# P transposes of every second macro step as pairs of 64-row tiles beside the K transposes, in a two-block cached attention kernel

## The chip, the cores and the metric

The kernel runs on one core of one Trainium2 chip. The metric is the device time of one execution in microseconds (us); lower is better. Three executions of the kernel before took 855.37, 857.67 and 857.76 us, median 857.67.

A core has a matrix engine (TensorE, PE; its weight loads are shown apart as PEld), a vector engine (VectorE, DVE), a scalar engine (ScalarE, ACT), GpSimd (POOL) and SyncE (SP), which here issues the loads. PSUM is the memory that TensorE writes; the kernel uses it as 8 banks of 512 fp32 (or 1024 bf16) per partition.

## The reference

Two independent attention blocks A and B, with the same shapes and all inputs in bf16; their outputs are joined along the last axis.

```
B, Sq, D = 16, 64, 640 ;  H, Sk, Dh = 32, 512, 128
q      = (x @ wq).reshape(B, Sq, H, Dh).transpose(0, 2, 1, 3)
scores = einsum("bhqd,bhkd->bhqk", q, k_cache) * Dh ** -0.5
p      = softmax(scores, axis=-1)
o      = einsum("bhqk,bhkd->bhqd", p, v_cache)
out    = o.transpose(0, 2, 1, 3).reshape(B, Sq, H * Dh) @ wo
```

The K and V caches of the two blocks, four arrays of 64 MB, make nearly all of the 297 MB that the DMA engines move.

## The kernel before

**Tiling.** Two batches (64 queries each) stand together on the 128 partitions. A *step* g is one head of such a batch pair; a *macro step* m is two steps (two heads), and there are 256 of them; a *pair* is two macro steps, m even and m odd, and there are 128. Heads are worked on in four passes of 16 heads (two per block), each over 8 batch pairs.

**Kinds of operations.** Each operation of the plan has a short name; `em_<name>` emits its instructions.

- KX (TensorE) transposes the K tile of a macro step: 32 transposes of 64-row tiles, alternating between partitions 0 to 63 and 64 to 127 and between two PSUM banks (6 and 7). KE (DVE) copies both banks to SBUF.
- QJ, QZ, QN (TensorE) compute the projected queries, 5 matmuls over 640 = 5 x 128; QEJ, QEZ, QEN (ACT) copy them out. QZ is for the first pass over the heads, QN for the rest; the last 16 pairs have none.
- SM (TensorE) computes the scores of one step, in bank 2 + g % 4. MX (DVE) takes the row maximum, EX (ACT) the exponential with the row sum, RC2 (DVE) two reciprocals, NM (POOL) the normalised P of one step in bf16 (`pn_ring`).
- TR2 (TensorE) transposes the normalised P of a macro step, 2 steps x 4 column tiles: 8 transposes of 128x128 into one bank, `TRB[m % 2]`, so bank 2 for even and bank 3 for odd macro steps. TA2 (ACT, even m) or TE2 (DVE, odd m) copies the 1024 columns to `pT_ring`.
- PV2 (TensorE) multiplies with V, 16 matmuls of 64 columns, each for one batch (j), step (sub) and column tile (t), in bank 1; OE4 (ACT) copies a pair's result out.
- OP2 and OX (TensorE) multiply with `wo`, 512 and 128 output columns, in banks 0 and 4; OX runs every fourth pair for 16 heads' worth of its small columns. OVP, OXP (ACT) and OVF, OXF (DVE) copy or add the sums, ST stores. XT and XTE transpose x of block B, through bank 4.

Banks 2 to 5 are thus shared: scores, P transposes (2 and 3), OX and XT (4).

**Order.** It is written out by hand as a table. `PHASES` has four phases, from pair 0, 16, 112 and two before the end, and for each engine (TensorE, ACT, DVE, POOL) a list of entries (kind, offset in macro steps, sub, time within a period). `build_plan` gives each operation the time stamp m - offset + 2 t / PERIOD and sorts every engine's list by it; a template's times order the work and are no durations. Dependencies are found from the resources (banks and ring slots) that an operation reads and writes, in the order of the time stamps, and become semaphore waits; `prune_waits` drops those that another one implies.

**Loads.** All K, V and weight loads are issued by SP in one list. `LEAD` and `WLEAD` say how many macro steps ahead of its first use a load is wanted, and `STEP_US`, `DMA_US`, `START_US` and `BEFORE` turn the plan into a pace: each load waits for the TensorE operation that this pace puts beside it. K has a ring of 9 macro steps, V one of 5 pairs; each of the two V loads of a pair is 512 KB, as is each K load.

In the steady part of the plan (pairs 16 to 111), TensorE's order in a pair is SM x4, KX, QN, TR2 x2 (16 transposes), OP2 x2 (4 matmuls), KX, PV2 x2, with OX or XT between OP2 and the second KX where they occur.

Lines of the kernel before that the profile names: L550 K transposes, L557 their copy, L567 Q, L596 scores, L605 maxima, L621 exponentials, L627 reciprocals, L635 normalisation, L644 P transposes, L651 and L656 their copies by DVE and ACT, L666 PV, L681 and L691 output matmuls.

Of the kernel before, what the change touches and what calls it, by code (L numbers as in the profile page):

```python
# [15 lines left out]
class Cfg:  # L16
# [6 lines left out]
    LEAD = 4.68  # L23
    WLEAD = 4.56
    STEP_US = ((8, 39.85), (32, 17.16), (256, 3.11))
    DMA_US = dict(LDK=1.40, LDV=1.44, LDWQ=1.8, LDWO=1.8, LDX=1.3, LDXR=0.5)
    START_US = -168.79
    BEFORE = 1.75
# [17 lines left out]
          ("QEZ", 0, 1, 2.19), ("QEJ", 2, 0, 2.79), ("EX", 1, 0, 3.02), ("QEN", -6, 0, 3.12), ("TA2", -2, 0, 3.58),  # L46
          ("QEZ", 0, 2, 4.2), ("EX", 1, 1, 4.36), ("XTE", 8, 0, 4.4), ("QEZ", 0, 3, 4.6), ("QEZ", 0, 4, 4.7),
          ("OVP", -3, 0, 5.0), ("QEZ", 0, 5, 5.61), ("OXP", -3, 0, 5.75), ("QEZ", 0, 6, 5.9), ("QEZ", 0, 7, 6.3)),
# [10 lines left out]
          ("QEN", -6, 0, 3.35), ("TA2", -2, 0, 3.59), ("EX", 1, 1, 4.45), ("OXP", -3, 0, 4.84), ("OVP", -3, 0, 4.86),  # L59
          ("XTE", 0, 0, 4.88)),  # L60
         (("KE", 3, 0, 0.04), ("RC2", -1, 0, 0.64), ("MX", 0, 0, 0.87), ("MX", 0, 1, 1.32), ("MX", 1, 0, 1.41),
          ("MX", 1, 1, 1.55), ("KE", 2, 0, 2.37), ("RC2", 0, 0, 3.49), ("TE2", -1, 0, 4.58), ("OXF", -3, 0, 5.55),
          ("OVF", -3, 0, 5.65)),
# [21 lines left out]
    )  # L85
    TRB = (2, 3)
    OXB = 4
    OXH = False
    KTB = (6, 6)
# [23 lines left out]
def build_plan(dims, cfg):  # L113
# [72 lines left out]
    def make_op(kind, m, sub, ts):  # L186
# [64 lines left out]
        if kind in ("TE2", "TA2"):  # L251
            return mk("dve" if kind == "TE2" else "act", kind, m, [], [bank(cfg.TRB[m % 2]), ("pT", m % cfg.NT)], ts)
# [631 lines left out]
```

## Time and profile before

| | before |
|---|---|
| median of three executions | 857.67 us |
| the profiled execution, time / span | 857.66 / 855.9 us |
| PE, DVE, ACT, POOL busy | 805.9, 726.6, 633.0, 418.0 us |
| moved by DMA | 297.13 MB, mean 347 GB/s |
| K transposes, L550 | 8192, PE busy 167.4 us |
| P transposes, L644 | 2048, PE busy 137.4 us |
| granted TensorE clock | 1.00 |

The span is the time from the first to the last instruction; the execution's own time has 1.8 us around it. A line of costly groups reads: source line, engine, operation, output <- inputs, shapes, count | busy us, mean ns of one | idle time of the engine before them, and what ended it. A line of the timeline reads: start and length in us, engine, line, operation, tiles, shapes, count, and in brackets an idle stretch before it. Matmuls overlap in a pipeline, so the length of one (about 190 to 390 ns) is more than what it adds; what a group adds is the distance from its start to that of the next group. Some matmul records are missing from the trace: 497 of 512 for L681, for instance.

### The profile page before, as it was taken

What the parts mean: (1) busy time and instruction counts of PE and PEld (TensorE: products, weight loads), DVE (VectorE), ACT (ScalarE), POOL (GpSimd) and SP (SyncE); (2) the same over time, 40 slices, a digit from 0 to 9 for tenths busy, and PEclk for the clock granted to TensorE, in tenths of its full rate; (3) what the DMA queues carried; (4) which work ended last, traced back from release to release, by engine and by line L of the source; (5) the groups of instructions that cost most, each with busy time, mean ns of one, the idle gap of its engine ahead of it and who ended that gap; (6) DMA issues with size and microseconds to landing.
All of it is one profiled execution on the core that took longest, in us unless ns stands there. A gap on an engine that the chain in (4) does not pass through costs nothing.

```text
span 855.9 us, 38296 instructions
## 1 busy us (share of the span) xinstructions
PE 805.9 (94%) x16953; PEld 561.8 (66%) x17084; DVE 726.6 (85%) x1184; ACT 633.0 (74%) x1450; POOL 418.0 (49%) x518
## 2 busy tenths in 40 slices
PE   5999999999999999999999899999999999999987
PEld 3566666666666766766666666666676666666665
DVE  3588888898888899898898788988888889889995
ACT  2677787787787777777777777777877867767775
POOL 0344554545544554554554445555455545446554
DMA  8999999999999999999999999999999999999993
GB/s 266 321 368 367 357 352 328 358 352 346 356 363 354 355 364 366 359 368 369 366 354 368 316 355 364 360 358 362 355 363 364 364 360 370 346 307 350 368 352 115
DMA packets 232581, 297.13 MB, mean 347 GB/s; under 512 B 14304, under 2 KB 166880, under 8 KB 232416
## 3 DMA queue, kind: packets, MB, share of 16 engines
q1 hardware_dynamic: 230112, 292.06, 100.2%
q8 instruction: 133, 2.18, 1.1%
q10 hardware_dynamic: 2304, 2.62, 0.9%
q14 instruction: 32, 0.26, 0.1%
HBM read 290.72 MB, written 2.62 MB: 343 GB/s over the span
## 4 chain that ended last, share of the span: by engine, by line
PE 81%; DMA 9%; DVE 3%; issue 3%; ACT 2%; POOL 1%; SPq 1%; POOLq 0%; ACTq 0%; DVEq 0%
PE ps L550 15%; PE ps L567 14%; PE ps L666 14%; PE ps L596 13%; PE ps L644 11%; PE ps L681 11%; DMA v_ring<-in_B_v_cache_dram 6%; PE ps L691 3%; DMA v_ring<-in_A_v_cache_dram 3%; DVE ktp_ring L557 2%; DVE negmax L605 1%; POOL pn_ring L635 1%; ACT p_ring L621 1%; DMA wq_sb<-in_A_wq_dram 1%; ACT pT_ring L656 1%
## 5 line engine op out<-in xcount | busy, mean ns | idle before, releaser
L635 POOL TENSOR_SCALAR pn_ring<-p_ring,recip 128x512 bf16<-128x512 bf16 x512 | 417.4, 846 | 429.9 <-DVE recip L627 403.2
L621 ACT ACTIVATE p_ring<-ps,negmax 128x512 bf16<-128x512 f32 x512 | 350.0, 689 | 77.5 <-DVE negmax L605 74.3
L557 DVE COPY ktp_ring<-ps 128x2048 bf16<-128x2048 bf16 x256 | 311.9, 1218 | 78.6 <-PE ps L550 78.3
L605 DVE TENSOR_REDUCE negmax<-ps 128x1 f32<-128x512 f32 x512 | 320.6, 683 | 19.7 <-PE ps L596 12.6
L550 PEld LDWEIGHTS ps<-ident,kn_ring 64*128 64x128 bf16 x8192 | 135.8, 95 | 99.2 <-issue 58.8
L550 PE MATMUL ps<-ident,kn_ring 64*128 64x64 bf16 x8192 | 167.4, 191 | 5.3 <-DVE ktp_ring L557 2.6
L673 ACT ACTIVATE oT_ring<-ps 128x512 bf16<-128x512 f32 x128 | 76.4, 597 | 123.7 <-PE ps L666 123.7
L567 PE MATMUL ps<-xT_sb,wq_sb 128*128 128x512 bf16 (+2 forms) x544 | 135.7, 376 | 26.8 <-issue 18.3
L666 PE MATMUL ps<-pT_ring,v_ring 128*128 128x64 bf16 x4096 | 142.7, 193 | 7.4 <-DMA v_ring<-in_B_v_cache_dram 4.1
L644 PEld LDWEIGHTS ps<-ident,pn_ring 128*128 128x128 bf16 x2048 | 124.9, 98 | 34.8 <-ACT p_ring L621 3.4
L644 PE MATMUL ps<-ident,pn_ring 128*128 128x128 bf16 x2048 | 137.4, 219 | 1.7 <-POOL pn_ring L635 1.2
L596 PE MATMUL ps<-ktp_ring,qc_ring 128*64 128x512 bf16 x1024 | 137.6, 387 | 1.2 <-issue 1.1
L666 PEld LDWEIGHTS ps<-pT_ring,v_ring 128*128 128x128 bf16 x4096 | 127.4, 98 | 15.9 <-DMA v_ring<-in_B_v_cache_dram 5.3
L681 PE MATMUL ps<-wo_sb,oT_ring 128*128 128x512 bf16 x497 | 132.1, 379 | 5.0 <-ACT pT_ring L656 2.5
L656 ACT ACTIVATE pT_ring<-ps 128x1024 bf16<-128x1024 bf16 x128 | 132.6, 1036 | 0.6 <-PE ps L644 0.4
L621 ACT ACTIVATION_READ_ACCUMULATOR p_ring<-ps,negmax 128x1 f32 x512 | 105.2, 206 | 0.0
L567 PEld LDWEIGHTS ps<-xT_sb,wq_sb 128*128 128x128 bf16 x660 | 54.9, 99 | 62.8 <-DMA wq_sb<-in_A_wq_dram 7.7
L651 DVE COPY pT_ring<-ps 128x1024 bf16<-128x1024 bf16 x128 | 86.3, 674 | 6.9 <-PE ps L644 6.8
L583 ACT ACTIVATE qc_ring<-ps 128x512 bf16<-128x512 f32 (+1 forms) x129 | 77.1, 597 | 14.2 <-PE ps L567 14.2
L596 PEld LDWEIGHTS ps<-ktp_ring,qc_ring 128*64 128x64 bf16 x1024 | 47.3, 109 | 37.4 <-issue 5.0
L681 PEld LDWEIGHTS ps<-wo_sb,oT_ring 128*128 128x128 bf16 x512 | 43.4, 98 | 31.8 <-ACT pT_ring L656 4.6
L627 DVE RECIPROCAL recip<-rowsum 128x2 f32<-128x2 f32 x256 | 39.9, 156 | 9.1 <-ACT p_ring L621 9.1
(16 smaller groups left out, 109.1 us busy)
## 6 DMA issues: line engine op xcount, KB each, us to landing
kn_ring<-in_A_k_cache_dram SPq DMA_DIRECT2D x128, 512.0 KB, 6.7
v_ring<-in_A_v_cache_dram SPq DMA_DIRECT2D x128, 512.0 KB, 6.6
kn_ring<-in_B_k_cache_dram SPq DMA_DIRECT2D x128, 512.0 KB, 6.4
v_ring<-in_B_v_cache_dram SPq DMA_DIRECT2D x128, 512.0 KB, 6.3
wq_sb<-in_A_wq_dram SPq DMA_DIRECT2D x8, 640.0 KB, 6.6
wo_sb<-in_A_wo_dram SPq DMA_DIRECT2D x8, 640.0 KB, 6.8
wq_sb<-in_B_wq_dram SPq DMA_DIRECT2D x8, 640.0 KB, 6.4
wo_sb<-in_B_wo_dram SPq DMA_DIRECT2D x8, 640.0 KB, 7.4
```

Source lines behind the costliest of these rows:

```text
L550: last = e.transpose(kt_ps[hs][:, 64 * t:64 * t + 64], kn_ring[r, m % NKB, t // 8, t % 8 * DH:(t % 8 + 1) * DH], ident[r, r])
L557: ins = e.tensor_copy(ktp_ring[:, ktslot(op.idx)], ps[:, b:b + 2, :].rearrange("p b s -> p (b s)").bitcast(BF16))
L567: last = e.matmul(dst[:, col:col + n], wq_sb[:, qslot(hh // G), kt, (hh % G) * DH:(hh % G + 1) * DH], xT_sb[:, kt, lo * 128:hi * 128], sta ...
L596: ins = e.matmul(s_bank(g)[64 * j:64 * j + 64, :], q[:, 64 * j:64 * j + 64], kt[:, sub, j], start=True, stop=True, tile_position=(0, 64 * j))
L605: ins = e.reduce_max(negmax[:, r:r + 1], s_bank(g), axis=AX.X, negate=True)
L621: ins = e.activation(p_ring[:, g % NP, :], s_bank(g), ACTF.Exp, bias=negmax[:, r:r + 1], scale=1.0, accum_out=rowsum[:, r:r + 1])
L635: ins = e.tensor_scalar(dst, src, recip[:, r:r + 1], 1.0, ALU.mult, ALU.mult)
L644: ins = e.transpose(pt_flat(m)[:, (4 * sub + t) * 128:(4 * sub + t + 1) * 128], pn_ring[:, g % NPN, t * 128:(t + 1) * 128], ident[:, :])
L651: ins = e.tensor_copy(pT_ring[:, m % NT].rearrange("p s t q -> p (s t q)"), pt_flat(m))
L656: ins = e.activation(pT_ring[:, m % NT].rearrange("p s t q -> p (s t q)"), pt_flat(m), ACTF.Copy)
L666: ins = e.matmul(qo_ps[:, col:col + 64], v_ring[:, m // 2 % NVP, j, 2 * (m % 2) + sub, t * DH:(t + 1) * DH], pT_ring[:, m % NT, sub, t, 64 ...
L681: ins = e.matmul(out_ps, oT_ring[:, m // 2 % NO, 2 * (m % 2) + sub, :], wo_sb[:, wslot(ps_, hh // G), hh % G, 0:N0], start=(hh == 0), stop ...
```

## The change

Three things change.

First, `TRB` becomes `((2,), (3, 4))`. For even macro steps nothing changes. For odd ones a P transpose of 128x128 becomes two transposes of 64 rows, one per batch j, with a 64x64 identity: sixteen in place of eight. Batch 0 goes to bank 3 and batch 1 to bank 4, each half a bank. The DVE copy (TE2) reads both half banks as one access pattern and writes `pT_ring` batch by batch; PV2 reads it in that layout for odd m.

Second, the four phases of `PHASES` are written anew. In the steady part TensorE's order in a pair is now SM x4, KX, QN, TR2 (even, 8 transposes), OP2 (2 matmuls), TR2 (odd, 16 half transposes), KX, OP2 (2 matmuls), PV2 x2, with OX and XT between the last OP2 and PV2. DVE's order becomes KE, MX, RC2, MX, MX, KE, MX, TE2, RC2, where it was KE, RC2, MX x4, KE, RC2, TE2. ACT keeps three EX, QEN, TA2, EX, OE4. POOL's four normalisations are permuted.

Third, the constants of the loads' pace change, and at the very start a K tile is loaded and transposed ahead of the first x and wq. Two kinds that no phase uses (MX2 and RC4) are removed.

```diff
-    LEAD = 4.68
-    WLEAD = 4.56
-    STEP_US = ((8, 39.85), (32, 17.16), (256, 3.11))
+    LEAD = 4.6
+    WLEAD = 4.51
+    STEP_US = ((8, 47.78), (32, 9.16), (256, 3.09))
...
-    START_US = -168.79
-    BEFORE = 1.75
+    START_US = -120.72
+    BEFORE = 2.51
...
         (16,
-         (("SM", 0, 0, 0.0), ("SM", 0, 1, 0.21), ("SM", 1, 0, 0.43), ("SM", 1, 1, 0.64), ("KX", 2, 0, 1.42),
-          ("QN", -6, 0, 2.07), ("TR2", -2, 0, 2.96), ("TR2", -1, 0, 3.76), ("OP2", -4, 0, 3.83),
-          ("OP2", -3, 0, 3.98), ("XT", 0, 0, 4.35), ("OX", -3, 0, 4.75), ("KX", 5, 0, 4.88), ("PV2", -2, 0, 5.52),
-          ("PV2", -1, 0, 6.09)),
...
+         (("SM", 0, 0, 0.0), ("SM", 0, 1, 0.21), ("SM", 1, 0, 0.43), ("SM", 1, 1, 0.64), ("KX", 2, 0, 1.03),
+          ("QN", -6, 0, 2.41), ("TR2", -2, 0, 3.07), ("OP2", -4, 0, 3.1), ("TR2", -1, 0, 3.81), ("KX", 5, 0, 4.31),
+          ("OP2", -3, 0, 4.65), ("OX", -3, 0, 5.14), ("XT", 0, 0, 5.48), ("PV2", -2, 0, 5.49), ("PV2", -1, 0, 6.14)),
...
-    TRB = (2, 3)
+    TRB = ((2,), (3, 4))
...
-            return mk("pe", "TR2", m, [("pn", g0 % cfg.NPN), ("pn", g1 % cfg.NPN), ("ident",)], [bank(cfg.TRB[m % 2])],
-                      ts)
+            return mk("pe", "TR2", m, [("pn", g0 % cfg.NPN), ("pn", g1 % cfg.NPN), ("ident",)],
+                      [bank(b) for b in cfg.TRB[m % 2]], ts)
...
+        def pt_bank(m):
+            b = cfg.TRB[m % 2]
+            return ps[:, b[0]:b[-1] + 1, :].bitcast(BF16)[:, :, 0:8 * 128 // len(b)]
+
+        def pt_copy(m):
+            return pT_ring[:, m % NT].rearrange("p (b c) -> p b c", b=len(cfg.TRB[m % 2]))
...
             for sub in range(2):
-                g = 2 * m + sub
                 for t in range(4):
-                    ins = e.transpose(pt_flat(m)[:, (4 * sub + t) * 128:(4 * sub + t + 1) * 128], pn_ring[:, g % NPN, t * 128:(t + 1) * 128], ident[:, :])
...
+                    src = pn_ring[:, (2 * m + sub) % NPN, t * 128:(t + 1) * 128]
+                    for j in range(2 if pairs else 1):
+                        n = 64 if pairs else 128
+                        r = slice(n * j, n * j + n)
+                        c = (4 * sub + t) * n
+                        last = e.transpose(dst[:, j, c:c + n], src[r], ident[r, r])
+                        first = first or last
...
-            ins = e.tensor_copy(pT_ring[:, m % NT].rearrange("p s t q -> p (s t q)"), pt_flat(m))
+            ins = e.tensor_copy(pt_copy(op.idx), pt_bank(op.idx))
...
-                                       pT_ring[:, m % NT, sub, t, 64 * j:64 * j + 64], start=(t == 0), stop=(t == 3))
+                                       pT[:, sub, t, j], start=(t == 0), stop=(t == 3))
```

More of the change, by code (lines that the diff above doesn't have):

```diff
@@ L236, in make_op @@
             return mk("act", kind, idx, [], [bank(b)] + [("qc", c_) for c_ in cells], ts, aux=cells)
-        if kind == "MX2":
-            return mk("dve", "MX2", m, [], [bank(2 + g0 % cfg.NS), bank(2 + g1 % cfg.NS), ("negmax", r0), ("negmax", r1)],
-                      ts)
-        if kind == "RC4":
-            rs = [g % cfg.NR for g in range(4 * k, 4 * k + 4)]
-            return mk("dve", "RC4", k, [("rowsum", r) for r in rs], [("recip", r) for r in rs], ts)
         if kind == "SM":
@@ L517, in mha_kernel @@
         pn_ring = sb("pn_ring", [128, NPN, SK], BF16)
-        pT_ring = sb("pT_ring", [128, NT, 2, 4, 128], BF16)
+        pT_ring = sb("pT_ring", [128, NT, 2 * 4 * 128], BF16)
         oT_ring = sb("oT_ring", [128, NO, 4, 128], BF16)
@@ L639, in em_TR2 @@
             m = op.idx
+            pairs = len(cfg.TRB[m % 2]) > 1
+            dst = pt_bank(m)
             first = last = None
             for sub in range(2):
-                g = 2 * m + sub
                 for t in range(4):
-                    ins = e.transpose(pt_flat(m)[:, (4 * sub + t) * 128:(4 * sub + t + 1) * 128], pn_ring[:, g % NPN, t * 128:(t + 1) * 128], ident[:, :])
-                    first = first or ins
-                    last = ins
+                    src = pn_ring[:, (2 * m + sub) % NPN, t * 128:(t + 1) * 128]
[5 more added lines that the diff above has]
+                        first = first or last
             return first, last
         def em_TE2(e, op):
-            m = op.idx
-            ins = e.tensor_copy(pT_ring[:, m % NT].rearrange("p s t q -> p (s t q)"), pt_flat(m))
+            ins = e.tensor_copy(pt_copy(op.idx), pt_bank(op.idx))
             return ins, ins
         def em_TA2(e, op):
-            m = op.idx
-            ins = e.activation(pT_ring[:, m % NT].rearrange("p s t q -> p (s t q)"), pt_flat(m), ACTF.Copy)
+            ins = e.activation(pt_copy(op.idx), pt_bank(op.idx), ACTF.Copy)
             return ins, ins
@@ L660, in em_PV2 @@
             m = op.idx
+            pT = pT_ring[:, m % NT]
+            if len(cfg.TRB[m % 2]) > 1:
+                pT = pT.rearrange("p (j s t q) -> p s t j q", j=2, s=2, t=4)
+            else:
+                pT = pT.rearrange("p (s t j q) -> p s t j q", j=2, s=2, t=4)
             first = last = None
```

34 lines of the change are left out of this document (12 added, 22 removed), and 58 rows, old and new, of the table PHASES.

## The prediction

> **What bounds the kernel now.** I read the busy table first, then the chain of work that ended last, the costliest groups, the order of time inside one repetition, and last the long stretch of repetitions in one window.
>
> ```profile
> span 855.9 us, 38296 instructions
> PE 805.9 (94%) x16953; PEld 561.8 (66%) x17084; DVE 726.6 (85%) x1184; ACT 633.0 (74%) x1450; POOL 418.0 (49%) x518
> PE 81%; DMA 9%; DVE 3%; issue 3%; ACT 2%; POOL 1%; SPq 1%; POOLq 0%; ACTq 0%; DVEq 0%
> L550 PEld LDWEIGHTS ps<-ident,kn_ring 64*128 64x128 bf16 x8192 | 135.8, 95 | 99.2 <-issue 58.8
> L644 PEld LDWEIGHTS ps<-ident,pn_ring 128*128 128x128 bf16 x2048 | 124.9, 98 | 34.8 <-ACT p_ring L621 3.4
> ```
>
> TensorE (PE) is busy 94% of the span and is 81% of the chain, with DMA second at 9%. The two weight-load rows are for the K transposes (L550, 64-row tiles) and the P transposes (L644, full tiles).
>
> One repetition (two macro steps, a "pair") in order of time, with TensorE alone:
>
> ```profile
> 428.56 1.05 PE L596 MATMUL ps<-ktp_ring,qc_ring 128*64 128x512 bf16 x8
> 429.55 0.64 PE L550 MATMUL ps<-ident,kn_ring 64*128 64x64 bf16 x32
> 430.35 1.03 PE L567 MATMUL ps<-xT_sb,wq_sb 128*128 128x512 bf16 x4 [0.16 <-issue]
> 431.21 1.06 PE L644 MATMUL ps<-ident,pn_ring 128*128 128x128 bf16 x16
> 432.10 1.03 PE L681 MATMUL ps<-wo_sb,oT_ring 128*128 128x512 bf16 x4
> 433.06 0.64 PE L550 MATMUL ps<-ident,kn_ring 64*128 64x64 bf16 x32
> 433.64 1.11 PE L666 MATMUL ps<-pT_ring,v_ring 128*128 128x64 bf16 x32
> 434.67 0.62 PE L596 MATMUL ps<-ktp_ring,qc_ring 128*64 128x512 bf16 x4
> ```
>
> Start to start, a pair takes 434.67 - 428.56 = 6.11 us with no hole. (The Q row shows 4 of its 5 matmuls; the 0.16 stands where a record is missing, since 429.55 + 0.57 + 5 x 0.218 = 431.21.) Of it 16 P transposes take 432.10 - 431.21 = 0.89, so 55.6 ns each, and 32 K transposes 433.64 - 433.06 = 0.58 or, in the chain, 0.57: 17.8 ns each, every one with a weight load of its own.
>
> ```profile
> 52.70:730.80 678.10, 653.14 (x13901) 458.53 (x14003) 593.49 (x966) 519.49 (x1195) 342.85 (x420) 1.00 1.04 358
> 360.00:420.00 60.00, 58.06 (x1240) 41.16 (x1248) 53.35 (x88) 46.90 (x108) 30.74 (x38) 1.00 1.07 368
> 730.80:846.00 115.20, 105.81 (x2320) 74.23 (x2337) 105.73 (x179) 84.70 (x195) 60.81 (x76) 1.00 0.97 329
> PE ps L666 <- DMA v_ring<-in_B_v_cache_dram: 4.1, 7, 1.2
> PE ps L666 <- DMA v_ring<-in_A_v_cache_dram: 1.7, 3, 1.2
> ```
>
> Window rows give, after the length, busy time of PE, PEld, DVE, ACT and POOL, then clock, DMA share and GB/s. The first is the long middle: 105 pairs (L644 has 1680 instructions there, 16 a pair). PE is busy 653 of 678 us; V loads that have not landed hold PE for 4.1 + 1.7 = 5.8 us in it (the two wait rows, of the same window). DMA moves 358 GB/s x 678.1 us = 242.8 MB there; in the second window it holds 368 GB/s for 60 us. So the middle could not be shorter than 242.8 / 0.368 = 660 us: TensorE bounds it, with the transfers 18 us behind.
>
> **The change, part by part.**
>
> *P transposes of the odd step.* Eight 128x128 transposes (0.445 us) become sixteen of 64 rows. They have the shape of the K transposes: 64x128 weights, a 64x64 identity, alternating halves, two banks. At 17.8 ns they take 0.285: 0.16 us less a pair. The bounds: 0.285 if the halves overlap as K's do; 16 x 27.8 (half of 55.6) = 0.445, nothing saved, if they follow one another. I take K's rate, the same form beside them.
>
> The number of weight loads doubles, and a load of 64 rows takes 95 ns against 98 for 128 (the two L550 and L644 rows above). Eight more of them, if nothing hid them, would cost 8 x 0.095 = 0.76 us a pair, and the change would be a loss of 0.76 - 0.16 = 0.6. But 32 K loads pass in 0.57 us, so loads of this form overlap; I take 0 and keep the loss as a rival. The Trainium skill, "TensorE: Matmul & The Clock Gate", section "LDWEIGHTS (loading the stationary operand)", states it as a rule: a weight load's time goes by its columns, not its rows; the 95 and 98 ns agree, and by the rule without overlap the sum would be that loss.
>
> *Order on TensorE.* Now: scores, K, Q, 8 P, 2 output matmuls, 16 half P, K, the other 2, PV. There is still one passage from 512-column matmuls into 64-row tiles at this place: before, the output group takes 433.06 - 432.10 = 0.96 for 4 x 0.218, so the passage costs 0.09, and it only moves. Leaving K for output matmuls is new here; the last repetitions already do it with no hole (K at 790.43 + 0.57, two outputs 0.44, P at 791.44). So 0, at most 0.09 a pair. The new pair: 6.11 - 0.16 = 5.95.
>
> *Evacuation.* ACT's copy of the even step keeps form (1036 ns). DVE's 674 ns copy reads two half banks instead of one. Near row: K's copy reads two banks, 2048 elements in 1218 ns, no dearer per element. Far row: two 683 ns reductions of 512 fp32 = 1.37 us. I take 674. DVE per pair, start to start: 2 x 1.13 (K) + 2.38 (4 maxima) + 0.15 (2 reciprocals) + 0.6 = 5.4 of 5.95, still covered; it would stop being cover above some 1.15 us.
>
> *Waits that move.* Half P now needs banks 3 and 4, so exponentials 2 and 3 of the pair. These end 2.7 and 3.4 us after the first score matmul (430.58 + 0.68 and 431.24 + 0.69, less 428.56), and half P starts at 0.99 + 0.57 + 1.09 + 0.445 + 0.53 (two outputs and the passage) = 3.6: 0.2 in hand. K, two outputs and PV would queue behind it; I take 0, at most the 0.1 of the next wait. DVE does maximum 4 after a K copy instead of before, so exponential 4 comes later, but ACT does it after the pT copy anyway. That pT copy ends at 433.42, 0.22 before PV (433.64). PV now comes 0.16 earlier and ACT's chain 0.07 at most (a reciprocal moves behind the first maximum): 0.05 to 0.13 in hand. I take 0; the bound is 0.1 a pair, 10.5 us. The small output matmuls (26 groups of 0.89) lose the K group between them and the scores that reuse bank 4; DVE's 0.29 or ACT's 0.28 still fits before the third score matmul, 1.5 us later. POOL, half idle (342.85 of 678), only permutes its work: nothing.
>
> *SP's loads.* Order differs in the first 19 only: a K tile goes ahead of x and Wq. PE waited 7.7 us for Wq; it may wait 1.4 longer (512 KB at 368 GB/s), and may gain 0.96 of K transposes and a 1.32 us wait for their copy. I take 0, since transfers run at 366 GB/s until 100 us and set the pace. Leads and paces shift by some per cent; V loads land a median 6.5 us after issue, with a lead in steps that shrinks with the pair.
>
> *Last repetitions* (730.8 on): no Q, pairs at 5.49 us against 4.9 of PE work, DVE busy 105.7 of 115.2 us. They are not TensorE's: 0.
>
> *Sum.* 105 x 0.16 = 16.8. The middle falls to 661.3, against 660 for the transfers; with the cover down from 18 us to 1, V waits must grow. I give back half the present 5.8, so 3: middle 664.3, which is 365.5 GB/s. Span 855.9 - 16.8 + 3 = 842.1; the profiled execution took 857.66 (1.8 around the span), as good as the median 857.67. So **844 us**.
>
> **The rivals.**
>
> 1. The pT wait opens: PV finds ACT 0.1 late in every pair. 857.7 - 16.8 + 10.5 = 851.4. For it: the thin 0.05 to 0.13. Against: ACT is idle 23% of the middle.
> 2. Down to the transfer floor: new pacing removes the V waits, middle 660 (-18), and the waits for the pT copy at 742 and 749 us (0.56 and 0.74) go: 857.7 - 18 - 1.3 = 838. Against: 368 GB/s without a pause.
> 3. No change, 857.7, in one of three ways. The half tiles don't overlap (0.445 us; 0.05): against it stands K's rate. The two-bank copy goes to 1.2 us or more and DVE takes the place of PE (0.02). Or the transfers cannot average above the 358 GB/s of the middle, which then stays at 678 us (0.04): 368 over 60 us speaks against it. The Trainium skill, "DMA: Bandwidth & Descriptors", section "Specifications", gives about 358 GB/s as HBM's limit per core, and by that figure nothing would be won; the 60 us at 368 disagree.
> 4. Slower: V starvation. From 466 to 482 us three pairs in a row had V 0.9 to 1.2 us late. A pair of the middle takes 678.1 / 105 = 6.46 us on average and its transfers 660 / 105 = 6.29, so 0.17 us a pair refills the lead after such a spell; after the change 0.01 is left. If the lead stays empty, with one such wait of 1.2 us every 4 pairs, 26 in all, 31 us come on top: 857.7 - 16.8 + 31 = 872. It decides from 0.16 us of V wait a pair. For it: at 65.7 us, with DMA at 367 GB/s, PE already waited 0.37 for V. Against: a V wait itself lets DMA catch up.
> 5. Unhidden weight loads: 857.7 + 105 x 0.6 = 921. K's rate all but excludes it.
>
> **How the numbers follow.** Chances: forecast 0.45 (own range 839 to 849), rival 1 0.17, rival 2 0.10, rival 3 0.11, rival 4 0.16, rival 5 0.01. A change under 0.3%, 2.6 us, is about what a measurement here cannot tell from none. Faster: 0.45 + 0.17 + 0.10 = 0.72; same: 0.11; slower: 0.17. The range leaves out most of rival 4 and rival 5 (0.15) and the far end of rival 2, where the start gains too (0.04): 834 to 861.
>
> **What would show it.** Right: the 16 half P matmuls in 0.28 to 0.29 us, pairs of 5.95, the middle's DMA at 364 GB/s or above, V waits up a few us. Wrong: half P at 0.45; PV waiting for the pT copy in most pairs (rival 1); V waits over 20 us (rival 4); DVE's copy above 1 us (rival 3). What would make the forecast wrong as a whole is the start: the first loads are reordered, and the trace of before shows no such order.

## The result, and the profile after

| | before | after |
|---|---|---|
| median of 4 executions each, same chip | 856.52 us | 879.63 us |
| ratio, 95% interval | | 1.028 (1.024 to 1.031) |
| profiled execution, time / span | 857.66 / 855.9 us | 883.32 / 881.5 us |
| pairs 4 to 109 (the middle) | 678.1 us | 700.0 us |
| start / last repetitions | 52.7 / 125.1 us | 53.6 / 127.9 us |

The change costs 23 us; the forecast was a gain of 14. The profiled execution of after is 3.7 us above its median, and 60 us of it (480 to 520 and 580 to 600) ran at a granted clock of 0.91, so part of these 3.7 us may be the clock's. Of the 25.6 us between the two spans 21.9 lie in the middle.

The page of after, in the order of the lines shown of before (span, busy table, chain by engine, K weight loads, and from the answer by forms the weight loads of the half tiles):

```profile
span 881.5 us, 40136 instructions
PE 774.2 (88%) x17863; PEld 534.0 (61%) x18108; DVE 723.6 (82%) x1184; ACT 635.4 (72%) x1450; POOL 415.8 (47%) x518
PE 50%; ACT 21%; DMA 12%; DVE 8%; issue 6%; SPq 2%; ACTq 0%
L549 PEld LDWEIGHTS ps<-ident,kn_ring 64*128 64x128 bf16 x8192 | 139.8, 96 | 78.4 <-issue 72.4
...
L639 PEld LDWEIGHTS ps<-ident,pn_ring 64*128 64x128 bf16 x2048 | 37.5, 95 | 59.0 <-ACT p_ring L610 47.6 <-issue 10.0 <-ACT pT_ring L648 0.6
```

TensorE is recorded as busy for less time (774 against 806 us) and the span is longer: it waits. Some 18 of these 32 us are no work saved: 114 more matmul records are missing than in before (18108 - 17863 against 17084 - 16953), and each leaves a place of 0.16 us. In the chain ACT went from 2% to 21%, DMA from 9 to 12%, "issue" from 3 to 6%. The page counts 1840 instructions more.

The timeline of after, TensorE alone, one pair and the start of the next:

```profile
435.87 1.05 PE L595 MATMUL ps<-ktp_ring,qc_ring 128*64 128x512 bf16 x8
436.86 0.64 PE L549 MATMUL ps<-ident,kn_ring 64*128 64x64 bf16 x32
439.31 1.04 PE L566 MATMUL ps<-xT_sb,wq_sb 128*128 128x512 bf16 x4 [1.80 <-issue]
440.18 0.61 PE L639 MATMUL ps<-ident,pn_ring 128*128 128x128 bf16 x8
440.63 0.59 PE L678 MATMUL ps<-wo_sb,oT_ring 128*128 128x512 bf16 x2
441.15 0.41 PE L639 MATMUL ps<-ident,pn_ring 64*128 64x64 bf16 x16
441.40 0.63 PE L549 MATMUL ps<-ident,kn_ring 64*128 64x64 bf16 x32
442.19 0.38 PE L678 MATMUL ps<-wo_sb,oT_ring 128*128 128x512 bf16 x1 [0.16 <-issue]
442.40 1.10 PE L663 MATMUL ps<-pT_ring,v_ring 128*128 128x64 bf16 x32
443.43 1.05 PE L595 MATMUL ps<-ktp_ring,qc_ring 128*64 128x512 bf16 x8
```

The 16 half P transposes take 441.40 - 441.15 = 0.25 us, 15.6 ns each, where K's 32 take 0.57, 17.8 each. The tiles are no faster than K's: within a group both follow each other at 14.5 ns, and K's 0.57 us holds some 0.1 us of passage into the full tiles behind it, which half P, with K right behind, does not have. But in this pair of 7.56 us TensorE stood still for 1.80 us ahead of Q, and nothing that the trace records released it ("issue"). The packet records of the DMA engines have what came just before: a packet of the instruction queue (16 KB) had landed 1.39 us before the end of that hole. In the table of the DMA queues for the stretch from 436.70 to 438.00 us (packets, MB, share of 16 engines) it is this line:

```profile
q8 instruction: 1, 0.02, 5.5%
```

The middle in one window (columns as before), then TensorE's waits in it (total us, times, longest), then two queues of the page, and last the instruction queue of the page of before:

```profile
53.60:753.60 700.00, 625.74 (x14635) 436.31 (x14843) 590.23 (x964) 522.36 (x1195) 339.40 (x419) 0.99 1.02 346
...
PE ps L678 <- ACT pT_ring L648: 18.7, 60, 0.6
PE ps L566 <- issue: 18.5, 105, 1.8
PE ps L549 <- issue: 10.3, 17, 1.8
PE ps L663 <- DMA v_ring<-in_B_v_cache_dram: 9.2, 10, 2.5
PE ps L663 <- DMA v_ring<-in_A_v_cache_dram: 3.4, 3, 1.3
PE ps L678 <- issue: 8.7, 45, 1.7
...
q1 hardware_dynamic: 230112, 292.06, 98.3%
q8 instruction: 141, 2.31, 1.1%
...
q8 instruction: 133, 2.18, 1.1%
```

Three waits grew.

- **V loads**: 9.2 + 3.4 = 12.6 us, against 5.8 before.
- **The pT copy of ACT**: 60 pairs. Each of these lines also covers 0.16 us of a missing matmul record (the first of the two L678 matmuls is missing in every pair, as the timeline shows), so 18.7 - 60 x 0.16 = 9 us are waiting.
- **"issue"**: the places of missing records (0.16 us each) make most of the short ones, so I count those of 0.19 us or more: 32 with 19.5 us, against 4 with 1.7 us before. Of the 32, 30 end between 1.1 and 1.75 us after an instruction packet has landed; packets come every 6 us or so, hence chance would put one in ten there. I call these 30 (18.9 us) *fetch stalls* below.

That is 7 + 9 + 17 = 33 us more, against 105 x 0.20 = 21 saved in the half tiles: 12 of the 21.9. The other 10 lie in stretches too short to name and, as far as the profiled run goes, in the lower clock.

The page of after has 141 instruction packets where before has 133. By the Trainium skill, "Perfetto Trace Analysis", section "The 4-stage abstract model", an instruction has 64 bytes. As an estimate from that, 16 more a pair (8 transposes, 8 weight loads) are 105 x 1 KB = 6.6 packets in the middle. The trace agrees: its records show 116 there for 110.

The trace also has a sharper sign than the distance from a packet. Over the whole run the half tiles add 8 transposes and 8 weight loads to each of 128 pairs, 2048 instructions, for 8 more packets: 256 to a packet, or 128 weight loads with their matmuls. In all 30 fetch stalls of after, the number of weight loads begun when the hole opened is 95 more than a multiple of 128; for the two other holes it is 104 and 40. So whenever TensorE stalls, it does so at one and the same place of its 256 instructions, whatever operation stands there, and goes on soon after a packet has landed. Before's 4 stalls stand at the same 95.

### The profile page after: what moved, and what is told of

Read it like the earlier page. It is cut to its first block, busy times and chain, and to the rows that moved or that the text cites. A ratio compares the mean times of both kernels' runs of the same rounds, so it can differ in the third digit from the quotient of the medians.

```text
span 881.5 us, 40136 instructions
## 1 busy us (share of the span) xinstructions
PE 774.2 (88%) x17863; PEld 534.0 (61%) x18108; DVE 723.6 (82%) x1184; ACT 635.4 (72%) x1450; POOL 415.8 (47%) x518
## 4 chain that ended last, share of the span: by engine, by line
PE 50%; ACT 21%; DMA 12%; DVE 8%; issue 6%; SPq 2%; ACTq 0%
ACT p_ring L610 13%; PE ps L663 12%; DMA v_ring<-in_B_v_cache_dram 9%; PE ps L595 8%; PE ps L566 8%; PE ps L549 7%; PE ps L678 7%; DVE negmax L604 5%; ACT pT_ring L648 5%; PE ps L639 5%; ACT qc_ring L582 3%; PE ps L688 3%; DMA v_ring<-in_A_v_cache_dram 2%; DVE ktp_ring L556 2%; SPq L761 1%
## 5 line engine op out<-in xcount | busy, mean ns | idle before, releaser
L604 DVE TENSOR_REDUCE negmax<-ps 128x1 f32<-128x512 f32 x512 | 334.2, 682 | 93.9 <-PE ps L595 93.6
L549 PE MATMUL ps<-ident,kn_ring 64*128 64x64 bf16 x8192 | 171.3, 191 | 20.6 <-issue 14.4
L549 PEld LDWEIGHTS ps<-ident,kn_ring 64*128 64x128 bf16 x8192 | 139.8, 96 | 78.4 <-issue 72.4
L639 PEld LDWEIGHTS ps<-ident,pn_ring 64*128 64x128 bf16 (+1 forms) x3072 | 104.7, 96 | 90.0 <-ACT p_ring L610 49.3
L566 PE MATMUL ps<-xT_sb,wq_sb 128*128 128x512 bf16 (+2 forms) x544 | 136.4, 377 | 25.3 <-issue 19.8
L663 PEld LDWEIGHTS ps<-pT_ring,v_ring 128*128 128x128 bf16 x4096 | 135.2, 98 | 33.9 <-DMA v_ring<-in_B_v_cache_dram 12.3
L678 PE MATMUL ps<-wo_sb,oT_ring 128*128 128x512 bf16 x383 | 125.7, 382 | 33.4 <-ACT pT_ring L648 19.5
L639 PE MATMUL ps<-ident,pn_ring 64*128 64x64 bf16 (+1 forms) x3072 | 132.0, 201 | 5.8 <-ACT p_ring L610 4.1
L644 DVE COPY pT_ring<-ps 128x1024 bf16<-128x1024 bf16 x128 | 88.4, 691 | 19.7 <-PE ps L639 19.4
L582 ACT ACTIVATE qc_ring<-ps 128x512 bf16<-128x512 f32 x129 | 76.9, 596 | 29.4 <-PE ps L566 29.0
L566 PEld LDWEIGHTS ps<-xT_sb,wq_sb 128*128 128x128 bf16 x660 | 54.6, 100 | 62.8 <-issue 5.8
L678 PEld LDWEIGHTS ps<-wo_sb,oT_ring 128*128 128x128 bf16 x512 | 39.4, 97 | 33.0 <-ACT pT_ring L648 16.9
```

The source lines that it names most:

```text
L549: last = e.transpose(kt_ps[hs][:, 64 * t:64 * t + 64], kn_ring[r, m % NKB, t // 8, t % 8 * DH:(t % 8 + 1) * DH], ident[r, r])
L566: last = e.matmul(dst[:, col:col + n], wq_sb[:, qslot(hh // G), kt, (hh % G) * DH:(hh % G + 1) * DH], xT_sb[:, kt, lo * 128:hi * 128], sta ...
L582: last = e.activation(qc_ring[:, c[0]:c[-1] + 1:c[1] - c[0], :], src[:, i * 128:(i + n) * 128].rearrange("p (b q) -> p b q", b=n), ACTF.Co ...
L604: ins = e.reduce_max(negmax[:, r:r + 1], s_bank(g), axis=AX.X, negate=True)
L639: last = e.transpose(dst[:, j, c:c + n], src[r], ident[r, r])
L663: ins = e.matmul(qo_ps[:, col:col + 64], v_ring[:, m // 2 % NVP, j, 2 * (m % 2) + sub, t * DH:(t + 1) * DH], pT[:, sub, t, j], start=(t == ...
```

## The experiments

Times are medians; each run ran on one of three chips beside the kernel before, which took 856.1 to 857.9 us there, so a difference of two runs is good to some 2 us. The columns from "middle" on are those of the one profiled execution, which lies up to 4 us from its median. "Stalls" are fetch stalls, "V" the waits for V loads, "copy" those for the pT copy (places of missing records taken off), all in the middle, in us. Of the fifteen totals only those of e9, e13 and e15 fell inside a range that I had given, and e10 and e12 missed one by less than 0.5 us; the argument rests on differences between runs and on the waits in their traces.

| | what | median | ratio (95%) | middle | shortest / median pair | stalls | V | copy |
|---|---|---|---|---|---|---|---|---|
| before | | 856.5 | | 678.1 | 6.11 / 6.11 | 1.7 | 5.8 | |
| after | | 879.6 | 1.028 (1.024-1.031) | 700.0 | 6.06 / 6.34 | 18.9 | 12.6 | 9 |
| e1 | full tiles | 862.9 | 1.009 (1.006-1.012) | 682.5 | 6.11 / 6.11 | 1.3 | 9 | 0 |
| e5 | full tiles, old pace: order alone | 856.7 | 1.000 (0.998-1.002) | 677.4 | 6.11 / 6.11 | 1.5 | 5.4 | 0 |
| e3 | half tiles, old pace | 867.3 | 1.012 (1.009-1.015) | 680.4 | 6.06 / 6.18 | 12.8 | 5.2 | 10 |
| e6 | before, new pace | 873.2 | 1.018 (1.015-1.021) | 692.9 | 6.11 / 6.11 | 1.6 | 19.7 | |
| e2 | before, half tiles | 888.4 | 1.038 (1.035-1.040) | 700.4 | 6.11 / 6.33 | 4.3 | 2.8 | |
| e4 | after, half loads | 834.1 | 0.974 (0.972-0.976) | 658.5 | 6.06 / 6.06 | 0.9 | 0 | 11 |
| e13 | e1, half loads | 843.6 | 0.986 (0.984-0.988) | 668.1 | 6.11 / 6.11 | 0 | 0 | 0 |
| e7 | e1, 8 more instructions a pair | 890.1 | 1.037 (1.033-1.042) | 705.3 | 6.11 / 6.48 | 9.9 | 11.4 | 0 |
| e11 | e7, half loads | 856.5 | 1.001 (1.000-1.002) | 679.1 | 6.11 / 6.25 | 0.2 | 0 | |
| e12 | e3, 8 K transposes a pair less | 851.6 | 0.995 (0.993-0.997) | 672.6 | 6.06 / 6.11 | 6.1 | 6.6 | |
| e15 | e3, half as many half tiles | 863.0 | 1.009 (1.007-1.011) | 682.0 | 6.06 / 6.22 | 8.5 | 4.4 | 4.5 |
| e9 | before, loads earlier | 857.5 | 1.001 (0.999-1.002) | 677.0 | 6.11 / 6.18 | 3.3 | 1.8 | |
| e10 | e3, loads earlier | 866.8 | 1.013 (1.011-1.014) | 685.5 | 6.06 / 6.18 | 21.9 | 2.6 | |
| e8 | e3, copies swapped | 884.5 | 1.031 (1.028-1.034) | 696.7 | 6.03 / 6.47 | 24.6 | 3.3 | 6 (DVE) |
| e14 | e8, DVE's copy earlier | 881.5 | 1.030 (1.026-1.034) | 695.2 | 5.90 / 6.47 | 27.0 | 3.6 | 0 |

### Which part costs: tiles, order, pace

**e1: after without the half tiles.**

```diff
-    TRB = ((2,), (3, 4))
+    TRB = ((2,), (3,))
```

> The changed kernel with its new order and pace, and only the half tiles undone (eight full P transposes in the odd step too, bank 3). In the profile of the changed kernel three costs stand in the middle stretch of 105 pairs: TensorE waits of 18.7 us for the pT copy of ACT, 18.9 us in which TensorE ran out of nothing that a semaphore shows and went on 1.2 to 1.6 us after a packet of the instruction queue had landed, and 12.7 us for V loads. Theory A (instruction supply suffers from the half tiles, which add 16 instructions to the 258 of a pair and make TensorE burn through them faster): the instruction waits fall back to about 2 us, a pair is TensorE's again at 6.09, time 855 to 861. Theory B (the new order and pace do the damage, whatever the tiles): instruction and V waits stay above 25 us together, time 870 to 882.

862.9 us: 16.8 less than after, and still slower than before. The stalls go from 18.9 to 1.3. So the half tiles themselves are the larger part of the loss, and something else is lost too.

**e3: after with before's pace; e5: e1 with before's pace; e6: before with the new pace.** The edit is the same five constants each time (in e6 the other way round).

```diff
-    LEAD = 4.6
-    WLEAD = 4.51
-    STEP_US = ((8, 47.78), (32, 9.16), (256, 3.09))
+    LEAD = 4.68
+    WLEAD = 4.56
+    STEP_US = ((8, 39.85), (32, 17.16), (256, 3.11))
...
-    START_US = -120.72
-    BEFORE = 2.51
+    START_US = -168.79
+    BEFORE = 1.75
```

> The changed kernel with the five constants of the loads' pace as they were before. If the pace is what makes V late, the V waits of the middle fall from 12.7 us towards 6.1 and the time to 870 to 874, with the waits for the pT copy (18.7) and for instructions (18.9) where they are. If the pace is not the cause (V is late because TensorE runs ahead between its other waits, or because DMA has no spare), V waits stay at 10 to 15 us and the time within 876 to 883.

> The new order alone: eight full P transposes in the odd step, and the five constants of the loads' pace as before. Measured so far: changed kernel 879.6, its pace undone 867.3, its half tiles undone 862.9, before 856.3. If the two costs add (pace 12, half tiles 17), the order by itself gives 851 to 854, a little faster than before or the same. If the pace only hurts where half tiles speed TensorE up, this comes out at 860 to 863. In both cases the pair is 6.11 with waits for the pT copy of about 0.1 us inside it.

> The kernel before with only the five constants of the loads' pace of the changed one. If the pace by itself makes loads late, V waits in the middle rise from 6 to 10 us or more and the time is 860 to 868. If it hurts only with the new order, the time stays within 854 to 859.

The order alone costs nothing (856.7). Half tiles on top cost 867.3 - 856.7 = 10.6, and the pace 879.6 - 867.3 = 12.3: together the 23 of the change. In the old order the pace alone costs 873.2 - 857.9 (before, beside it) = 15.3, and its profile shows where. TensorE's waits in the middle of e6:

```profile
PE ps L567 <- issue: 16.7, 105, 0.2
PE ps L666 <- DMA v_ring<-in_B_v_cache_dram: 16.1, 13, 3.0
PE ps L666 <- DMA v_ring<-in_A_v_cache_dram: 3.6, 6, 1.0
```

V is 19.7 us late in all, where it was 5.8; everything else is as before. The plan's table fits this: for macro steps 136 to 160, where the leads are shortest, a K load is released on average 2.94 macro steps ahead of its first use in e6, where it was 3.55, and a V load 2.68 for 2.87 (2.95 and 2.74 in after); and 8 of e6's 19 V waits, with 10.5 us, stand at macro steps 134 to 150. (This lead is worked out from the table, from the TensorE operation that a load waits for; it is not measured.)

**e2: before's order with half tiles** (from macro step 34 on; DVE's copy sorted a little earlier).

```diff
-          ("MX", 1, 1, 1.55), ("KE", 2, 0, 2.37), ("RC2", 0, 0, 3.49), ("TE2", -1, 0, 4.58), ("OXF", -3, 0, 5.55),
+          ("MX", 1, 1, 1.55), ("KE", 2, 0, 2.37), ("RC2", 0, 0, 3.49), ("TE2", -1, 0, 4.3), ("OXF", -3, 0, 5.55),
...
-    TRB = (2, 3)
+    HALF_FROM = 34
+
+    def trb(self, m):
+        return (2,) if m % 2 == 0 else (3, 4) if m >= self.HALF_FROM else (3,)
...
```

The rest of the edit, left out here, is the code of after for half tiles.

> The kernel before, order and pace and constants included, with the half tiles of the odd step put in where they stood (right behind the full ones, output matmuls between them and the K transposes), from macro step 34 on; DVE's copy of them only gets an earlier time stamp, its place on DVE is the same. Theory A (half tiles hurt the instruction supply): instruction waits of 10 us or more in the middle and a time of 860 to 872, although a pair of TensorE work is 5.9 to 6.0. Theory B (the new order does it): instruction waits near the 1.7 us of before, pairs near 6.0 because the pT copy then holds PV by less than 0.1 us, time 846 to 854.

888.4 us, worse than after. In the timeline of e2 all 24 P transposes of a pair stand together, and take 395.56 - 394.46 = 1.10 us where 0.445 + 0.25 were to be had:

```profile
394.46 1.17 PE L644 MATMUL ps<-ident,pn_ring 128*128 128x128 bf16 x24
395.56 1.04 PE L683 MATMUL ps<-wo_sb,oT_ring 128*128 128x512 bf16 x4
...
L644 PE MATMUL ps<-ident,pn_ring 64*128 64x64 bf16 x1776 | 45.8, 191 | 25.1 <-ACT p_ring L615 10.7 <-POOL pn_ring L629 1.6 <-issue 1.2
```

Of the excess of 0.41 us some 0.2 are two passages, from full tiles into 64-row tiles and back, of 0.1 each; the other 0.22 are a wait for exponentials (`p_ring`), since bank 4 holds scores that the third exponential still reads. In at least three of four pairs the first half tile starts 54 to 55 ns after the end of that exponential; in after it starts 272 ns after it (median). In the middle it is mostly too short to be named in the row above: of its 10.7 us 8.8 lie in the last repetitions. Less the 0.20 saved in the tiles, pairs go from 6.11 to 6.33, 105 x 0.22 = 23 us. In the new order two output matmuls stand before the half tiles, and the waits named for exponentials are 3.6 us in the whole run. In the old order half tiles lose even without fetch stalls (4.3 us here).

### Why faster tiles lose time

**e4: after with half of each K and V load left out; e13: e1 with the same.** The rings keep older data in the other half, so that TensorE, DVE, ACT and POOL do the same work.

```diff
-                ins = e.dma_start(v_ring[:, m // 2 % NVP, m % 2], src)
+                n = G if m < 2 * NVP else G // 2
+                ins = e.dma_start(v_ring[:, m // 2 % NVP, m % 2, 0:n], src[:, 0:n])
...
-                ins = e.dma_start(kn_ring[:, m % NKB], src)
+                n = 2 if m < NKB else 1
+                ins = e.dma_start(kn_ring[:, m % NKB, 0:n], src[:, 0:n])
```

> The changed kernel, with half of each K and V load left out once the rings have been filled once (half of the batches of a K tile, half of the heads of a V tile), so the output is wrong and only the traffic differs. Theory A (instruction waits come from instruction fetches that queue behind a saturated DMA): instruction waits and V waits both go to about 2 us; what is left is the pT wait of 0.17 us a pair, middle near 700 - 17 - 12 = 671, time 845 to 852. Rival (TensorE's front end alone is too slow for the burst of 48 half tiles, whatever the transfers do): V waits go, instruction waits of 15 us and more stay, time 864 to 870.

> The order and pace of after with full P tiles (as e1), and half of each K and V load left out (that part of the computation is left out). Base for e4 and e11. Theory (instruction fetches of TensorE wait behind the loads): e1's 862.9 us loses its V waits and its few stalls, pairs stay at 6.11, 836 to 844 us; then half tiles without the traffic (e4, 834.1) are 2 to 10 us faster than full ones, and 16 further instructions a pair without the traffic (e11, 856.5) cost only their own length, 13 to 20 us. Rival (half tiles are themselves the loss, by their wait for the P copy): e4 would not be faster than this run, which would be 826 to 833 us.

Without the traffic half tiles are 843.6 - 834.1 = 9.4 us *faster*; with it they are 10.6 (old pace) to 16.8 (new pace) slower. So 20 to 26 us of the loss exist only beside the loads. The window of the middle and TensorE's waits there, e4 first:

```profile
51.90:710.40 658.50, 612.76 (x14634) 431.65 (x14845) 587.10 (x964) 519.60 (x1195) 340.27 (x420) 1.00 0.68 202
PE ps L678 <- ACT pT_ring L648: 23.1, 73, 0.5
PE ps L566 <- issue: 16.7, 105, 0.2
PE ps L678 <- issue: 5.1, 32, 0.2
```

and e13:

```profile
52.00:720.10 668.10, 634.29 (x13797) 467.28 (x14003) 593.09 (x964) 520.62 (x1195) 342.06 (x420) 1.00 0.68 198
PE ps L566 <- issue: 16.7, 105, 0.2
PE ps L678 <- ACT pT_ring L648: 12.0, 74, 0.4
PE ps L678 <- issue: 4.9, 31, 0.2
```

At 202 GB/s instead of 346 no "issue" wait is longer than 0.5 us, and what is left of them is one missing record a pair for L566 and for L678 (105 x 0.16 = 16.8; 73 or 74 x 0.16 = 12 under the copy's name). e4's 23.1 is 11 us more than that: the pT wait. With it the pair is 6.06, not 5.95 or, with the measured tile, 5.91.

**e7: e1 with a row of waits that are met already, ahead of the second half of each odd P transpose; e11: the same with half loads.** I wrote sixteen waits; the page counts 1024 instructions more than in e1, so 8 a pair, half of what half tiles add, with no change to any tile.

```diff
             for sub in range(2):
+                for _ in range(16 if m % 2 and sub else 0):
+                    e.wait_ge(sems[("s_init",)], 2)
```

> As the run with the half tiles undone (new order and pace, full tiles, 862.9, instruction waits 1.3 us in the middle), with 16 more TensorE instructions in each odd step: waits on a semaphore value that was reached at the start, put between the transposes of the two steps. So a pair has 274 instructions of TensorE, as with half tiles, but no half tiles. If the number of instructions is what the supply can't follow, instruction waits of 8 us or more come back (the changed kernel has 18.9) and the time is 868 to 880. If it is the burst of 48 short matmuls, they stay under 4 us and the time within 860 to 867, plus at most what the 16 waits take themselves.

> The run with full tiles and 16 more TensorE instructions a pair (890.1), with half of each K and V load left out once the rings are full (wrong output; only the traffic differs). It gives the price of the 16 instructions without the traffic. If they hurt because instruction fetches queue behind the loads, instruction waits go to about 1 us, pairs stay at 6.1 to 6.2 and the time is 840 to 852. If the 16 waits are slow in themselves, most of the 27 us stays: 865 or more.

Without traffic they cost 856.5 - 843.6 = 13.0 us, their own length. With it 890.1 - 862.9 = 27.3: another 14 us that belong to no tile or bank, and stalls after instruction packets again (13, with 9.9 us). In the profiled executions, whose middles differ by 22.8 us with traffic and 11.0 without, stalls (8.6 us more) and V waits (2.4 more) make 11.0 of the 11.8 left. TensorE's waits in the middle of e7:

```profile
PE ps L566 <- issue: 19.4, 105, 1.7
PE ps L680 <- issue: 10.5, 66, 0.2
PE ps L665 <- DMA v_ring<-in_B_v_cache_dram: 8.4, 10, 1.3
...
PE ps L549 <- issue: 5.2, 7, 1.5
```

**e12: e3 with 28 instead of 32 K transposes a macro step** (from step 6 on), so that a pair has as many instructions as before.

```diff
-            for t in range(16):
+            for t in range(16 if m < 6 else 14):
```

> The changed kernel with the pace of before (867.3), with 4 of the 32 K transposes of each macro step left out from the seventh on (wrong output). A pair then has 258 TensorE instructions, as before the change, while the half tiles and the order stay; ACT's chain of 6.06 us a pair isn't touched, so a pair doesn't get shorter by it. If the number of instructions is what the supply can't follow, instruction waits fall from 12.8 us to 4 or less and the time to 852 to 859. If it is the half tiles' burst, they stay at 9 us or more and the time at 863 to 868.

**e15: e3 with half tiles in every fourth macro step only.**

```diff
-    TRB = ((2,), (3, 4))
+
+    def trb(self, m):
+        return (2,) if m % 2 == 0 else (3, 4) if m % 4 == 1 else (3,)
+
...
```

> e3 (new order, before's pace, 867.3 us) with half tiles in every fourth macro step only, so half as many, 266 TensorE instructions a pair on average. Theory (the cost goes by instructions and by half-tile pairs): half of e3's excess over e5 (856.7), so 859 to 864 us, with 5 to 8 us of stalls after instruction packets in the middle stretch. Rival (the mode of a tile, once used, costs a fixed amount, or the loads set the time): 866 to 868 us as e3, or 855 to 857 us as e5.

e12 has half of e3's stalls left (6.1 for 12.8), between the two expectations (4 or less, 9 or more): the number of instructions is a part of the cause and, by this run, not all of it. It is 15.7 us faster, but the work that it leaves out is worth 105 x 8 x 17.9 ns = 15 us by itself, so its total says little; the stalls do. e15 takes 863.0, between e5's 856.7 and e3's 867.3, with 8.5 us of stalls between 1.5 and 12.8 (10.5, with a hole of 2.0 us that ends 1.86 us after its packet and stands at the same place of the 256 instructions): the cost goes with the number of half tiles.

| added instructions a pair | loss that exists only beside full loads |
|---|---|
| 8, no tile (e7 - e1, less e11 - e13) | 27.3 - 13.0 = 14 us |
| 8 on average, half tiles (e15 - e5, plus half of e13 - e4) | 6.3 + 4.7 = 11 us |
| 16, half tiles, old pace (e3 - e5, plus e13 - e4) | 10.6 + 9.4 = 20 us |
| 16, half tiles, new pace (after - e1, plus e13 - e4) | 16.8 + 9.4 = 26 us |

The stalls follow, roughly, the rate at which TensorE uses instructions up. A plain pair of before has 258 (matmuls and weight loads: 128 for K, 32 P, 64 PV, 16 scores, 10 Q, 8 output), so 42 per us in 6.11 us, with 1.7 us of stalls; e2's 274 in 6.33 make 43, with 4.3; after's 274 in 6.06 make 45, with 12.8 (e3), 18.9 and 21.9 (e10, below); e14's 274 in 5.90 (below) make 46, with 27.0. At 43 per us stalls range widely: 4.3 in e2, 6.1 in e12 (258 in 6.06) and 9.9 in e7 (266 in 6.11 to 6.25). So the rate alone does not set them.

### Can the loads or the copy be moved out of the way?

**e9 and e10: loads released earlier**, in before and in e3.

```diff
-    STEP_US = ((8, 39.85), (32, 17.16), (256, 3.11))
+    STEP_US = ((8, 39.85), (32, 17.16), (256, 3.2))
```

> The kernel before with one constant changed: the plan's time for a macro step, third entry of STEP_US, 3.20 in place of 3.11 (the changed kernel has 3.09). A load's place in the queue's plan then lags less behind its wanted lead, so loads go out earlier. If the lag of the plan is what made loads late in the run with the new pace alone (873), this goes the other way: V waits in the middle fall from 6 us towards 1 to 3 and the time to 850 to 855. If DMA has no more to give, or the earlier loads only stand longer in the queues and delay the instruction fetches, the time stays at 855 to 860.

> The changed kernel (new order, half tiles) with the pace of before (867.3) and the same constant at 3.20. If the V waits that are left (5.4 us in the middle) go, 861 to 865; instruction waits (12.8) and pT waits (19.7) stay. If earlier loads delay the instruction fetches further, those grow and the time is 867 or more.

Neither total moves. V waits fall (5.8 to 1.8, 5.2 to 2.6) and the stalls rise, in before by less than that (1.7 to 3.3), with half tiles by more (12.8 to 21.9). There, earlier loads buy V with instructions.

**e8: DVE copies the even P and ACT the odd one** (with half tiles and the old pace), to take the copy off ACT's chain; **e14: the same with DVE's copy ahead of the fourth maximum.**

```diff
-          ("TA2", -2, 0, 4.76), ("OVP", -3, 0, 5.63), ("EX", 1, 1, 5.85), ("XTE", 0, 0, 5.92), ("ST", -9, 0, 6.11),
+          ("TA2", -1, 0, 4.76), ("OVP", -3, 0, 5.63), ("EX", 1, 1, 5.85), ("XTE", 0, 0, 5.92), ("ST", -9, 0, 6.11),
...
-          ("KE", 2, 0, 1.85), ("MX", 1, 1, 4.16), ("TE2", -1, 0, 4.74), ("RC2", 0, 0, 5.47), ("OVF", -3, 0, 5.83),
+          ("KE", 2, 0, 1.85), ("TE2", -2, 0, 4.1), ("MX", 1, 1, 4.16), ("RC2", 0, 0, 5.47), ("OVF", -3, 0, 5.83),
...
```

> The changed kernel with the pace of before (867.3 so far), and the two pT copies swapped: DVE (0.67 us) takes the even step, whose pT PV needs first, and ACT (1.03 us) the odd step, which PV needs 0.5 us later. If ACT's chain is what holds a pair at 6.06, the pT waits (19.7 us in the middle) go and most pairs drop to 5.9; what is gained is then capped by the transfers (660 us for the middle), so instruction and V waits grow somewhat: time 850 to 860. If instruction supply and transfers set the middle anyway, the gain is eaten: 864 to 870, with pairs at 5.9 between longer waits. If ACT's copy now comes too late for the odd step, a wait of about the old size stands at the second half of PV.

> e8 (half tiles, before's pace, the DVE copying the half P and ACT the full one), with the DVE's P copy ahead of the fourth maximum, so that PV finds it in time. Theory (instruction supply and loads set the time once tiles are halved): the shortest pair falls to 5.9 to 6.0, stalls after instruction packets stay at 15 to 30 us in the middle stretch, and the whole takes 858 to 875 us, so not under the 856.5 of before. Rival (the late copy was the loss): the waits for the copy go, and the whole takes 842 to 853 us.

The diff is e14's against after, in the steady phase alone; the copies are swapped in the other phases too. In e8 TE2 stays at 4.74, behind the fourth maximum. There DVE's copy came some 0.11 us too late in half of the pairs, and the total, 884.5, is above every expected range. e14 mends that: pairs of 5.90 us, the pair that half tiles are worth, do occur. Two pairs of its timeline, one without and one with a stall:

```profile
308.46 1.05 PE L595 MATMUL ps<-ktp_ring,qc_ring 128*64 128x512 bf16 x8
...
313.34 1.10 PE L663 MATMUL ps<-pT_ring,v_ring 128*128 128x64 bf16 x32
314.36 1.05 PE L595 MATMUL ps<-ktp_ring,qc_ring 128*64 128x512 bf16 x8
315.35 0.64 PE L549 MATMUL ps<-ident,kn_ring 64*128 64x64 bf16 x32
316.15 0.81 PE L566 MATMUL ps<-xT_sb,wq_sb 128*128 128x512 bf16 x3 [0.16 <-issue]
317.97 0.39 PE L566 MATMUL ps<-xT_sb,wq_sb 128*128 128x512 bf16 x1 [1.01 <-issue]
...
321.45 1.05 PE L595 MATMUL ps<-ktp_ring,qc_ring 128*64 128x512 bf16 x8
```

314.36 - 308.46 = 5.90; the next takes 7.09, and its hole of 1.01 us lies in the middle of the five Q matmuls, where no operand is waited for. There are 37 stalls with 27.0 us, and a median pair of 6.47: the total is 881.5, above what I had expected for either theory. The faster TensorE becomes, the more it stalls, so the copy wait, though real, is not what a repair would have to remove first.

None of these kernels is faster than before with the whole work in it.

## Why the prediction was wrong, step by step

**Half P at K's rate, 0.16 us a pair.** Right, and too cautious: 0.25 instead of 0.285, so 0.20 saved. The rate of 17.8 ns, taken from K's 0.57 us, held the passage of 0.1 us behind K; with K right behind half P there is none. Rival 5 is refuted by the same line. 2048 weight loads of 64 rows take 95 ns each and all lie under other work; the part of the Trainium skill's rule that a load's time goes by columns, not rows ("TensorE: Matmul & The Clock Gate", "LDWEIGHTS (loading the stationary operand)") holds here, and the loss that it would mean without overlap did not come.

**Order at 0 to 0.09 a pair.** Right: 0.0 in e5.

**DVE's two-bank copy, 674 ns.** Right: 691, and 691 as well with one bank in the new order (e5).

**Waits of half P for the exponentials, 0.** Right: 3.6 us in the whole run. The "0.2 in hand" came from the two output matmuls ahead of it; without these (e2) the wait is 23 us.

**The pT copy, "0.05 to 0.13 in hand, I take 0".** Wrong, and rival 1's mechanism is there: the shortest pair is 6.06, where the tiles alone would give 5.91, 0.15 in place of a bound of 0.1. PV starts the next scores, these the maxima and exponentials, these the copy, and this the next PV: a ring of work. With the copies swapped (e14) pairs of 5.90 occur, so it is this ring that holds a pair at 6.06. A slack measured in one pair of before is no reserve when the whole ring has to become shorter. In the profile of before this showed only as 0.22 us between the copy's end and PV. By itself it would have left a gain: 9.4 us in e4.

**"Leads and paces shift by some per cent": 0.** The first step that failed. They cost 12.3 us here, 15.3 in the old order (e6), 6.2 with full tiles (e1 - e5). I knew of V waits of 5.8 us and had a rule (a load waits for the TensorE operation that the pace puts beside it), and could have compared each load's lead in the two plans, which is 0.6 macro steps (some 2 us) shorter for K in the tightest stretch.

**"Down to 661.3 against 660 for the transfers, give back 3."** The second step that failed, by a cause that I had not named. Rival 4 had the sign right (872, slower), but for another reason. What grew was not mainly V starvation (rival 4: 12.6 us instead of more than 20) but a wait for instructions: 18.9 us of fetch stalls, 12.8 with the old pace, where the sum had nothing. I priced the 16 extra instructions a pair only by their time on TensorE. Before's page and trace had both signs and I did not use them: the instruction queue among the DMA queues, and, over the whole run, seven "issue" holes of 0.35 to 0.93 us, each ending 1.3 to 1.6 us after a packet of that queue had landed.

**The transfer floor itself** was not reached by any kernel, but it is not 358 GB/s either: e12 moves 361 GB/s over its whole middle. The Trainium skill's figure ("DMA: Bandwidth & Descriptors", "Specifications"), which I had weighed, does not bound this core.

**What stays open.** That TensorE waits for instructions is shown by the one place in every 256 instructions at which the stalls stand (all of after, e3, e10 and e12; also e7, e8 and e14, to within one, when their recorded waits are counted as instructions), by their vanishing at half the traffic, and by e7. The delay lies ahead of the packets: they last about as long with half the loads (median 0.98 us in e4 against 1.09 in after), but they start later. Counted from the first weight load of the 256 instructions ahead of those that it brings, a packet starts at a median of 0.8 us in e13 and 0.9 in e4, at 2.5 in before and 3.05 in after; and no block is begun less than 1.2 us after its packet has landed. What delays the start, a request that queues behind the loads or something else, no record shows. And 10 of after's 21.9 us in the middle are not assigned to single waits.

## What to carry to other kernels

Where the DMA queues are full, count the instructions of an engine as traffic of their own: splitting tiles can make each faster and still lose, here about 1.3 to 1.8 us for each instruction added to a pair that runs 105 times. Look for "issue" holes in the profile of before, for what the instruction queue did 1 to 2 us ahead of their end, and for whether they stand at one place in every 256 instructions. A change of pacing constants is no detail: compare the lead of every load in the two plans, and the shortest one first.

## What the runs showed of the hardware

- A hole in TensorE's stream after an instruction packet ends 1.2 to 1.75 us after the packet has landed (median 1.39 in after, 1.46 in e14), whatever operation is next, even in the middle of a group. In after all 30 stand 95 weight loads behind a multiple of 128.
- Such holes become many only with both, more instructions and full queues. At 196 to 202 GB/s none to two of them are left in 105 pairs, whatever the tiles; at 350 to 358 GB/s with full tiles and no added waits there are two to six, and six at 346 with half tiles in the old order (e2); in the new order with half tiles or e7's waits, at 344 to 361 GB/s, there are 11 to 37.
- Transposes of 64-row tiles with alternating halves follow each other at 14.5 ns. Sixteen with the same kind behind them take 0.25 us; 32 of K with full tiles behind them take 0.57. The passage costs some 0.1 us each way: into 64-row tiles 0.09 behind the output matmuls, out of them 0.1 ahead of PV in before and of the output matmuls in e2.
